# A rewritten attention order, keys ahead of weights, and no repeated scores, in an attention and two-layer-expert kernel

## The chip, the cores and the metric

One core of one Trainium2 chip runs the kernel. The metric is the device time of one execution in microseconds (us); the median of 3 runs of the kernel before is 613.02 us (612.81 to 613.07). TensorE is PE in the profile, its weight loads PEld, VectorE DVE, ScalarE ACT, GpSimd POOL, and SyncE, which issues most transfers, SP.

## The reference

```
scores = (q @ k.T) / sqrt(64)             # 2 batches, 8 heads, 576 positions, 64 per head
keep a score where 0 <= row - column < 64
attn = exp(scores - max) / (sum + 1e-9)
x    = attn @ v                           # as 1152 rows of 512
out1 = sum over 4 experts of p[:, e] * (relu(x @ w1[e]) @ w2[e])      # 512 -> 1024 -> 512
out  = g(out1 @ w_in) @ w_out             # 512 -> 2048 -> 512, g(h) = max(h, 0) + alpha * min(h, 0)
```

## The kernel before, in words

Queries are handled in 18 blocks of 64 positions, all 8 heads at a time. Block j passes through steps, each named by a letter and the block in one long string, `TABLE` (L767): **S** multiplies queries by the keys of this block and the one ahead of it (`att_S`, L322, 16 PE instructions); **M** adds the mask and takes the row's maximum on DVE (`att_M`, L337); **E** is the exponential on ACT, four instructions that also leave the row sums (`att_E`, L344); **N** adds the sums, takes the reciprocal and scales (`att_N`, L349 to L353), the scaling on DVE for the blocks in `SCALE_V` and on POOL for the rest; **PT** transposes on PE and copies out of PSUM (`att_PT`, L360, the copy by DVE for the blocks in `COPY_V`, by ACT for the rest); **PV** multiplies by the values (`att_PV`, L377) and writes the result as a high and a low part, for the blocks in `DIRECT` by ACT and DVE, for the rest by a DVE copy and two POOL operations (L390, L391).

Every large product is made of three products of such high and low parts. **W_f** splits column block f of the first weights, the high part on ACT (L231), the low one on POOL (L232); **V_f** does so for the second weights on ACT and DVE (L222, L215). **L_c_f** is one piece of the first layer of expert 0 on row chunk c (`l1_chunk`, L521, 12 matmuls), **B_c_t** one piece of its second layer (`l2_chunk`, L554, 12 matmuls). The string sets the order on every engine: each engine gets its share of the steps in the order of the words, and executes them in that order. After the string come chunk 3 and all other expert halves; there PE's first product is `product` (L451).

Two things in it are there beside the reference's work. `repeat` (L300) issues scores that are overwritten afterwards, as `REPEAT = {("S", 1): 2, ("PT", 0): 6}` says: 8 matmuls ahead of S_1 and 12 ahead of PT_0 (L307). And the transfers at the start stand in one list (L696 to L716): SP issues queries, four value blocks, the first weights as one transfer of 1 MB (`load_w`, L147), then the other keys; ACT's queue issues the keys of blocks 0 to 3. A transfer on SP waits for the one eight before it to land.

Of the kernel before, what the change touches and what calls it, by code (L numbers as in the profile page):

```python
# [8 lines left out]
F32 = mybir.dt.float32  # L9
# [17 lines left out]
def tile_kernel(ctx, tc, q, k, v, probs, w1, w2, w_in, w_out, alpha, out):  # L27
    nc = tc.nc


    B, S, H, D = v.shape
    NP = H // 2
    NT, DM = out.shape
    E, _, F = w1.shape
    F2 = w_in.shape[1]
    BLK = 64
    GRP = 192
    GB = GRP // BLK
# [60 lines left out]
    for c in range(1, NCH):  # L99
        n = CHUNK[c + 1] - CHUNK[c]  # L100
# [3 lines left out]
    denom = [ab.tile([P, NP, 2], F32, name=f"su{i}") for i in range(4)]  # L104
# [11 lines left out]
    def keys(j):  # L116

        return BLK if j % NB == 0 else P

    def load_q(g, a=0, z=GB):  # L120
        b, i = divmod(g, S // GRP)
        nc.sync.dma_start(out=qs[g % 3][:, a:z], in_=q[b, i, :, a:z])

    def load_k(b, a, z, queue=nc.sync):
        queue.dma_start(out=kts[b][:, a:z], in_=k[b, :, a:z])

    def load_v(j):

        b, i = divmod(j, NB)
        t = ab.tile([P, H, D], F32, tag="v", bufs=6, name=f"v{j}")  # L130
        if i == 0:
            nc.sync.dma_start(out=t[0:BLK], in_=v[b, 0:BLK])
        else:
            nc.sync.dma_start(out=t, in_=v[b, BLK * (i - 1):BLK * (i + 1)])
        v_t[j] = t

    def load_w(tid):
        which, s = tid
        if which == 0:
            late["raw0"] = sb.tile([P, KD, LEN[0]], F32, tag="ws", bufs=2, name="xs0")  # L140
            return
        convert(NF * (2 * (s - S1) + which))
        t = sb.tile([P, 4, FS], F32, tag="ws", bufs=2, name=f"ws{which}_{s}")
        if s < S1:
            e, o = divmod(s, SPE)
            src = w1[e][:, o * FS:(o + 1) * FS] if which == 1 else w2[e][o * FS:(o + 1) * FS, :]
            nc.sync.dma_start(out=t, in_=src.rearrange("(k p) f -> p k f", p=P))  # L147
        else:
            nc.sync.dma_start(out=t, in_=conv[tid])
        ws_t[tid] = t  # L150
# [17 lines left out]
    A11, A12, A22, SA1, SA2, SA3, SA4 = range(7)  # L168

    def w_block(s, u, i, j):  # L170
        t = ws_t[1, s]
        if s >= S1:
            return t[:, 2 * u + i, 2 * j * P:2 * (j + 1) * P].rearrange("p (k m) -> p k m", k=2)
        c = (2 * u + i) * P
        return t[:, 2 * j:2 * j + 2, c:c + P]
# [16 lines left out]
    def w_split(s, u, part):  # L192
        if (s, u) not in wf_t:
            wf_t[s, u] = [late["wfp"].tile([P, 7, 2, P], F32R, tag=f"wf{w}", bufs=2, name=f"wf{w}_{s}_{u}") for w in "hl"]
        hi, lo = wf_t[s, u]
        if part == A11:
            n, t = 2, ws_t[1, s]
            src = (t[:, 2 * u, :].rearrange("p (k m) -> p k m", k=KD) if s >= S1 else t[:, :, 2 * u * P:(2 * u + 1) * P])
        elif part == A22:
            n, src = 1, w_block(s, u, 1, 1)  # L200
        else:
            n, src = 4, sr_t.pop((s, u)).rearrange("p o k m -> p (o k) m")
        split(*[x[:, part:part + n].rearrange("p o k m -> p (o k) m") for x in (hi, lo)], src)
# [137 lines left out]
    def att_E(j):  # L341
        (pt, st, sm), w = p_t[j], keys(j)
        for hp in range(NP):
            nc.scalar.activation(out=pt[:, hp, 0:w], in_=sm[:, hp, 0:w], func=AF.Exp, scale=-1.0,  # L344
                                 bias=st[:, 0, hp:hp + 1], accum_out=denom[j % 4][:, hp, 0:1])

    def att_N(j):
        (pt, st), w = p_t[j][0:2], keys(j)
        nc.vector.tensor_reduce(out=st[:, 1, :], in_=denom[j % 4], op=ALU.add, axis=AX.X)  # L349
        nc.vector.reciprocal(out=st[:, 2, :], in_=st[:, 1, :])  # L350
        x, y = pt[:, :, 0:w], st[:, 2, :].unsqueeze(2).to_broadcast([P, NP, w])
        e = nc.vector if j in SCALE_V else nc.gpsimd
        e.tensor_tensor(out=x, in0=x, in1=y, op=ALU.mult)  # L353
# [339 lines left out]
        nc.scalar.activation(out=raw2(p)[:, :, t * P:(t + 1) * P], in_=ps.rearrange("p (k t) -> p k t", k=KD), func=AF.Copy)  # L693

    with tc.manual_schedule():
        for g, x, y in ((0, 0, 1), (0, 1, GB), (1, 0, 1)):  # L696
            load_q(g, x, y)
            load_k(0, g * GB + x, g * GB + y, nc.scalar)
        for su in denom:
            nc.vector.memset(su[:, :, 1:2], 1e-9)  # L700
        make_mask()
        load_v(0)
        load_v(1)
        make_identity(nc, ident)
        load_v(2)
        load_v(3)
        load_w((1, 0))
        load_q(1, 1, GB)
        load_k(0, GB + 1, 2 * GB)
        load_k(0, 2 * GB, NB)  # L710
        load_q(2)
        load_w((2, 0))
        load_v(4)
        load_v(5)
        nc.sync.dma_start(out=praw, in_=probs)
        nc.sync.dma_start(out=alph, in_=alpha)  # L716
# [275 lines left out]
```

## Time and profile before

| | |
|---|---|
| median of 3 runs | 613.02 us (612.81 to 613.07) |
| span of the profiled execution, first to last instruction | 610.7 us |
| the median less that span, time around it | 2.3 us |
| PE busy in it | 603.0 us (99%) |
| DVE, ACT, POOL busy | 483.2, 322.8, 277.7 us |
| first matmul starts | 3.57 us |
| first `l1_chunk` matmul (L_0_0) starts | 18.17 us |
| first `product` starts, by the chain | 87.86 us |

Times within the execution count from the span's start. In a timeline or chain row the first number is the start, the second the duration, "xN" the number of merged instructions; a bracket tells how long the engine was idle before it and who ended that. [...]

### The profile page before, as it was taken

The page shows a single profiled execution, that of the slowest core. Times are in us where ns is not written, and L with a number is a line of the kernel's source. Part 1 is how long each engine was busy: PE and PEld are TensorE (multiplying, and loading weights), DVE is VectorE, ACT ScalarE, POOL GpSimd, SP SyncE. Part 2 cuts the span into 40 slices and gives each one's busy share as a digit, 9 for nine tenths or more (in the row PEclk, how much of TensorE's full clock was granted, in tenths as well). Part 3 has the DMA queues.
Part 4 walks back from the last instruction along what each step waited for, and adds up shares of the span by engine and source line. Part 5 has one row for each costly group of instructions (what it writes and reads, how often), then busy time and mean ns, then how long its engine had stood idle before and what let it go on. Part 6 is the DMA issues. An engine that isn't in the chain of part 4 may idle for free.

```text
span 610.7 us, 11051 instructions
## 1 busy us (share of the span) xinstructions
PE 603.0 (99%) x4096; PEld 548.4 (90%) x4096; DVE 483.2 (79%) x969; ACT 322.8 (53%) x805; POOL 277.7 (45%) x282
## 2 busy tenths in 40 slices
PE   7999999999999999999999999999999999999997
PEld 6998999889889889989989989989898988988987
DVE  5987497799798798798698698657968989766785
ACT  6975456436427426426515625536777653653750
POOL 4756411074253254265152452522755586664450
PEclk9999999999999999999999999999999999999999
DMA  8951005234234325324324323012302412310012
GB/s 321 329 201 36 1 1 170 72 105 164 97 103 156 94 96 172 106 71 171 104 95 150 120 87 104 17 70 80 128 1 78 152 48 80 119 45 1 2 52 105
DMA packets 31798, 62.61 MB, mean 103 GB/s; under 512 B 2432, under 2 KB 11904, under 8 KB 30720
## 3 DMA queue, kind: packets, MB, share of 16 engines
q1 hardware_dynamic: 31024, 61.25, 29.5%
q8 instruction: 32, 0.52, 0.4%
q10 hardware_dynamic: 720, 0.66, 0.3%
q14 instruction: 22, 0.18, 0.1%
HBM read 51.14 MB, written 10.75 MB: 101 GB/s over the span
## 4 chain that ended last, share of the span: by engine, by line
PE 98%; DMA 1%; DVE 1%; ACT 0%; POOL 0%; issue 0%; ACTq 0%; POOLq 0%
PE o L566 42%; PE X L451 23%; PE Z L451 12%; PE W L451 6%; PE h L521 4%; PE oc L554 4%; PE s L322 1%; PE pt L360 1%; PE pv L377 1%; PE mX L653 1%; PE x L692 1%; DMA kt<-in_k_dram 1%; PE mZ L653 0%; PE pt L307 0%; ACT p L344 0%; PE mW L653 0%
## 5 line engine op out<-in xcount | busy, mean ns | idle before, releaser
L566 PE MATMUL o<-w2h,hl 128*128 128x512 f32 x380 | 148.2, 390 | 0.0
L566 PE MATMUL o<-w2l,hh 128*128 128x512 f32 x380 | 148.2, 390 | 0.0
L566 PE MATMUL o<-w2h,hh 128*128 128x512 f32 x380 | 147.9, 389 | 0.0
L294 POOL TENSOR_TENSOR ct<-ct 128x512 f32<-128x512 f32 x32 | 44.3, 1383 | 117.9 <-DVE ct L293 53.6
L566 PEld LDWEIGHTS o<-w2h,hl 128*128 128x128 f32 x380 | 71.3, 188 | 15.8 <-POOL hl L547 0.7
L566 PEld LDWEIGHTS o<-w2l,hh 128*128 128x128 f32 x380 | 71.3, 188 | 14.2
L566 PEld LDWEIGHTS o<-w2h,hh 128*128 128x128 f32 x380 | 71.3, 188 | 14.2
L678 DVE SCALAR_TENSOR_TENSOR acc<-o,pn,acc 128x512 f32<-128x512 f32 x63 | 47.1, 747 | 38.9 <-PE o L566 38.7
L190 POOL TENSOR_TENSOR sr<-ws 128x256 f32<-128x256 f32 x44 | 41.0, 932 | 72.6 <-DVE wfl L215 61.5
L215 DVE SCALAR_TENSOR_TENSOR w2l<-ws,w2h 128x512 fp32r<-128x512 f32 x48 | 44.4, 935 | 17.9 <-ACT w2h L222 17.8
L451 PE MATMUL X<-xth,wfl 128*128 128x256 f32 (+1 forms) x264 | 56.8, 296 | 0.0
L451 PE MATMUL X<-xth,wfh 128*128 128x256 f32 (+1 forms) x264 | 56.6, 295 | 0.0
L451 PE MATMUL X<-xtl,wfh 128*128 128x256 f32 (+1 forms) x264 | 56.6, 295 | 0.0
L222 ACT ACTIVATE wfh<-sr 128x1024 fp32r<-128x1024 f32 x22 | 23.2, 1059 | 53.5 <-POOL sr L190 53.5
L295 POOL TENSOR_TENSOR ct<-ct 128x512 f32<-128x512 f32 x32 | 47.3, 1478 | 2.5
L282 ACT ACTIVATE ct<-wd 128x512 f32<-128x512 f32 x32 | 21.3, 667 | 47.7 <-DVE ct L288 47.7
L451 PEld LDWEIGHTS X<-xth,wfl 128*128 128x128 f32 x264 | 42.6, 190 | 0.0
L451 PEld LDWEIGHTS X<-xth,wfh 128*128 128x128 f32 x264 | 42.6, 190 | 0.0
L451 PEld LDWEIGHTS X<-xtl,wfh 128*128 128x128 f32 x264 | 42.6, 190 | 0.0
L451 PE MATMUL Z<-xth,wfl 128*128 128x320 f32 (+1 forms) x176 | 37.8, 296 | 0.0
L451 PE MATMUL Z<-xth,wfh 128*128 128x320 f32 (+1 forms) x176 | 37.7, 296 | 0.0
L451 PE MATMUL Z<-xtl,wfh 128*128 128x320 f32 (+1 forms) x176 | 37.7, 296 | 0.0
(209 smaller groups left out, 1426.1 us busy)
## 6 DMA issues: line engine op xcount, KB each, us to landing
ws<-in_moe_w_dram SPq DMA_DIRECT2D x16, 1024.0 KB, 5.9
wd<-in_moe_w_in_dram SPq DMA_DIRECT2D x16, 512.0 KB, 4.0
cv<-ct SPq DMA_DIRECT2D x32, 256.0 KB, 2.4
wd<-in_moe_w_out_dram SPq DMA_DIRECT2D x16, 512.0 KB, 3.6
ws<-cv SPq DMA_DIRECT2D x8, 1024.0 KB, 5.1
v<-in_v_dram SPq DMA_DIRECT2D x16, 256.0 KB, 5.7
out_dram<-acc SPq DMA_DIRECT2D x7, 256.0 KB, 2.0
q<-in_q_dram SPq DMA_DIRECT2D x4, 384.0 KB, 6.6
```

The lines of the kernel that those rows point to most:

```text
L190: e.tensor_tensor(out=t4[:, o], in0=x, in1=y, op=op)
L215: nc.vector.scalar_tensor_tensor(out=lv, in0=src, scalar=1.0, in1=hv.bitcast(F32), op0=ALU.mult, op1=ALU.subtract)
L222: nc.scalar.activation(out=hv, in_=src, func=AF.Copy)
L282: nc.scalar.activation(out=a, in_=top.bitcast(F32), func=AF.Abs, scale=LIFT)
L294: nc.gpsimd.tensor_tensor(out=y, in0=y, in1=e, op=ALU.mult)
L295: nc.gpsimd.tensor_tensor(out=y, in0=r, in1=y, op=ALU.add)
L322: nc.tensor.matmul(sv[hp][c, 0:w].rearrange("p (n t) -> p n t", t=BLK), lhsT=qs[g % 3][r, jb, hp, :], rhs=kts[b][r, lo:i + 1, hp, :], star ...
L451: nc.tensor.matmul(ps, lhsT=w[:, d, :], rhs=x[:, d, :], start=(first and m == 0), stop=(m == 5), skip_group_check=True)
L521: nc.tensor.matmul(ps, lhsT=w[:, d * P:(d + 1) * P], rhs=x[:, d, :], start=(m == 0), stop=(m == 3 * KD - 1))
L554: nc.tensor.matmul(ps, lhsT=h_c[c, f][a][:, t * P:(t + 1) * P], rhs=w_t[2, 0, f][b], start=(n == 0), stop=(n == 3 * NF - 1))
L566: nc.tensor.matmul(ps, lhsT=h_t[s, p, f][a][:, t * P:(t + 1) * P], rhs=w_t[2, s, f][b][:, cols], start=(n == 0), stop=(n == 3 * NF - 1))
L678: nc.vector.scalar_tensor_tensor(out=at, in0=ps, scalar=sc, in1=at, op0=ALU.mult, op1=ALU.add)
```

## The change

The order of the steps is a new string. No matmul is repeated. The sets are new: the scaling in N is on DVE for 11 blocks where it was for 4, the copy after PT on DVE for 5 where it was 6, `DIRECT` has 7 blocks where it had 9. For blocks 4, 13, 14 and 16 (`REDUCED`) ACT's exponentials leave no sums, and DVE adds 128x512 numbers in one instruction. The low part of W_3 is made by DVE. The transfers at the start follow a list of words: keys of blocks 4 and 5 come ahead of the weights, and the first weights in three pieces of 1, 1 and 2 column blocks. For that `w1` is laid out anew ahead of the launch, so that each column block of 128 stands in one run in each partition, as the weights of the last four stages already do.

```diff
-    COPY_V = (0, 1, 2, 4, 10, 12)
-    DIRECT = (0, 2, 3, 7, 11, 14, 15, 16, 17)
-    REPEAT = {("S", 1): 2, ("PT", 0): 6}
-    SCALE_V = (13, 14, 15, 17)
+    COPY_V = (0, 6, 13, 14, 15)
+    DIRECT = (2, 3, 5, 10, 11, 13, 16)
+    REPEAT = {}
+    SCALE_V = (0, 2, 3, 5, 9, 10, 12, 13, 15, 16, 17)
+    REDUCED = (4, 13, 14, 16)
+    LOW_V = (3,)
...
+    PIECES = ((0, 1), (1, 2), (2, 4))
+    def load_piece():
+        o, i = pieces.pop(0)
+        nc.sync.dma_start(out=o, in_=i)
...
+            if tid == (1, 0) and PIECES:
+                for f0, f1 in PIECES:
+                    pieces.append((t[:, f0:f1], src[:, f0:f1]))
...
-        src = ws_t[1, 0][:, :, f * P:(f + 1) * P]
+        src = ws_t[1, 0][:, f].rearrange("p (k m) -> p k m", k=KD)
         nc.scalar.activation(out=hv, in_=src, func=AF.Copy)
-        nc.gpsimd.tensor_tensor(out=lv, in0=src, in1=hv.bitcast(F32), op=ALU.subtract)
+        if f in LOW_V:
+            low(lv, src, hv)
+        else:
+            nc.gpsimd.tensor_tensor(out=lv, in0=src, in1=hv.bitcast(F32), op=ALU.subtract)
...
-                                 bias=st[:, 0, hp:hp + 1], accum_out=denom[j % 4][:, hp, 0:1])
+                                 accum_out=None if j in REDUCED else denom[j % 4][:, hp, 0:1])
...
+        if j in REDUCED:
+            nc.vector.tensor_reduce(out=denom[j % 4][:, :, 0:1], in_=pt[:, :, 0:w], op=ALU.add, axis=AX.X)
...
+        HEAD = "p_0_0_1 p_0_1_3 q_1_1_3 v_0 k_4_6 p_1_0_1 v_1 v_2 w q_2 w v_3 k_6_9 w v_4 u v_5 r"
...
-            "S_0 S_1 M_0 S_2 S_3 E_0 M_1 E_1 N_0 M_2 N_1 M_3 E_2 N_2 E_3 PT_0 PT_1 N_3 PV_0 W_0 PV_1 W_1 "
+            "S_0 S_1 M_0 E_0 S_2 M_1 N_0 E_1 M_2 E_2 N_1 PT_0 S_3 S_4 M_3 E_3 N_2 S_5 N_3 PT_1 PV_0 W_0 M_4 PT_2 "
```

On PE, between S_2 and the first value product. Before (the first two rows are the end of S_3, then the 12 repeated scores into PT_0's bank):

```order
L322 MATMUL s_0_208<-kt_103,q_110 64x128 x2
L322 MATMUL s_1_209<-kt_103,q_110 64x128 x2
L307 MATMUL pt_264<-kt_103,q_109 64x128 x12
L360 MATMUL pt_264<-ident,p_193 64x128 x4
L360 MATMUL pt_283<-ident,p_224 128x128 x4
L377 MATMUL pv_293<-ptr_281,v_137 64x64 x8
```

With the change (the first two rows are the end of S_2; of S_3, S_4 and S_5 one row of four each stands here):

```order
L333 MATMUL s_0_196<-kt_103,q_109 64x128 x2
L333 MATMUL s_1_197<-kt_103,q_109 64x128 x2
L373 MATMUL pt_234<-ident,p_187 64x128 x4
L333 MATMUL s_0_241<-kt_103,q_110 64x128 x2
L333 MATMUL s_0_251<-kt_103,q_110 64x128 x2
L333 MATMUL s_0_275<-kt_103,q_110 64x128 x2
L373 MATMUL pt_288<-ident,p_208 128x128 x4
L390 MATMUL pv_295<-ptr_239,v_141 64x64 x8
```

PT_0 now follows S_2 directly, and S_3, S_4 and S_5 stand behind it; S_0 to S_8, PT_0 to PT_3 and PV_0 to PV_3 are done ahead of the first L piece in both.

On POOL, its work up to the low part of W_2. Before:

```order
L353 TENSOR_TENSOR p_193<-p_193,st_192 128x4x64
L353 TENSOR_TENSOR p_224<-p_224,st_223 128x512
L353 TENSOR_TENSOR p_238<-p_238,st_237 128x512
L353 TENSOR_TENSOR p_248<-p_248,st_247 128x512
L232 TENSOR_TENSOR w1l_0_308<-ws_0_149,w1h_0_307 128x512
L390 CAST xah_80<-xr_84 128x4x64
L391 TENSOR_TENSOR xal_81<-xr_84,xah_80 128x4x64
L232 TENSOR_TENSOR w1l_1_326<-ws_0_149,w1h_1_325 128x512
L353 TENSOR_TENSOR p_367<-p_367,st_366 128x512
L232 TENSOR_TENSOR w1l_2_415<-ws_0_149,w1h_2_414 128x512
```

With the change:

```order
L366 TENSOR_TENSOR p_208<-p_208,st_207 128x512
L403 CAST xah_80<-xr_84 128x4x64
L404 TENSOR_TENSOR xal_81<-xr_84,xah_80 128x4x64
L243 TENSOR_TENSOR w1l_0_310<-ws_0_114,w1h_0_309 128x512
L403 CAST xah_80<-xr_84 128x4x64
L404 TENSOR_TENSOR xal_81<-xr_84,xah_80 128x4x64
L243 TENSOR_TENSOR w1l_1_388<-ws_0_114,w1h_1_387 128x512
L243 TENSOR_TENSOR w1l_2_406<-ws_0_114,w1h_2_405 128x512
```

Three of the four first scalings left POOL; two blocks' split into a high and a low part came to it, and the low parts of W_1 and W_2 stand behind each other.

On SP, the transfers of the start with the change (ws is the first weights, kt the keys):

```order
L124 DMA q_109<-in_q_dram 128x512
L124 DMA q_110<-in_q_dram 128x512
L134 DMA v_141<-in_v_dram 64x512
L127 DMA kt_103<-in_k_dram 128x512
L124 DMA q_110<-in_q_dram 128x256
L136 DMA v_146<-in_v_dram 128x512
L136 DMA v_148<-in_v_dram 128x512
L144 DMA ws_0_114<-in_moe_w_dram 128x512
L124 DMA q_111<-in_q_dram 128x768
L144 DMA ws_0_114<-in_moe_w_dram 128x512
L136 DMA v_153<-in_v_dram 128x512
L127 DMA kt_103<-in_k_dram 128x768
```

Before, the queries of block 3 (128x256) were the third transfer, and the keys of blocks 4 and 5 came behind the whole of ws.

## Rows read from the trace of the kernel before

**Rows 1.** The page: busy time of each engine, PE in 40 slices.
```profile
PE 603.0 (99%) x4096; PEld 548.4 (90%) x4096; DVE 483.2 (79%) x969; ACT 322.8 (53%) x805; POOL 277.7 (45%) x282
...
PE   7999999999999999999999999999999999999997
...
PEclk9999999999999999999999999999999999999999
```
**Rows 2.** Busy time by stretch (us of each engine, then granted clock).
```profile
0.00:88.00 88.00, 83.38 (x991) 74.71 (x992) 63.23 (x274) 59.18 (x211) 44.48 (x61) 1.00 0.44 154
```
**Rows 3.** The chain that ended last, 0 to 20 us (start, us, what).
```profile
1.18 3.67 DMA kt<-in_k_dram
...
4.89 3.10 PE s L322 x48
7.99 2.20 PE pt L307 x24
10.19 0.57 PE pt L360 x4
...
10.79 1.28 DVE ptr L364 x2
...
12.49 1.05 POOL p L353
...
13.59 0.66 PE pt L360 x4
...
15.32 1.66 ACT p L344 x8
...
18.17 1.66 PE h L521 x12
```
**Rows 4.** The same chain, 20 to 48 us: pieces of PE back to back.
```profile
20.27 2.88 PE h L521 x24
23.15 0.44 PE pt L360 x4
23.58 1.43 PE h L521 x12
25.02 1.08 PE pv L377 x32
...
27.95 1.11 PE s L322 x32
```
**Rows 5.** The same chain, 80 to 100 us.
```profile
87.86 1.43 PE X L451 x12
```
**Rows 6.** PE's groups by shape, 0 to 9.7 us (busy us, mean ns; idle before).
```profile
L322 PE MATMUL s<-kt,q 64*64 64x128 f32 x48 | 3.1, 425 | 0.2 <-DMA kt<-in_k_dram 0.2
```
**Rows 7.** PE's groups by shape, 9.7 to 88 us.
```profile
L322 PE MATMUL s<-kt,q 64*64 64x128 f32 x208 | 7.1, 274 | 0.0
```
**Rows 8.** DVE's timeline at N_0, 6.0 to 7.6 us.
```profile
6.91 0.16 DVE L349 TENSOR_REDUCE st<-su 128x4 f32<-128x8 f32 x1
7.10 0.18 DVE L350 RECIPROCAL st<-st 128x4 f32<-128x4 f32 x1
```
**Rows 9.** POOL's timeline, 7 to 22 us.
```profile
7.43 0.61 POOL L353 TENSOR_TENSOR p<-p,st 128x256 f32<-128x256 f32 x1 [4.44 <-DVE st L350]
8.60 1.04 POOL L353 TENSOR_TENSOR p<-p,st 128x512 f32<-128x512 f32 x1 [0.55 <-DVE st L350]
...
13.49 1.28 POOL L232 TENSOR_TENSOR w1l<-ws,w1h 128x512 fp32r<-128x512 f32 x1
14.71 0.40 POOL L390 CAST xah<-xr 128x256 fp32r<-128x256 f32 x1
15.19 0.73 POOL L391 TENSOR_TENSOR xal<-xr,xah 128x256 fp32r<-128x256 f32 x1
```
**Rows 10.** DVE's, then ACT's groups by shape, 0 to 70 us.
```profile
L353 DVE TENSOR_TENSOR p<-p,st 128x512 f32<-128x512 f32 x4 | 2.9, 712 | 0.1
...
L387 DVE COPY xr<-pv 128x256 f32<-128x256 f32 x9 | 3.7, 415 | 0.0
...
L344 ACT ACTIVATE p<-sm,st 128x128 f32<-128x128 f32 x64 | 24.8, 389 | 0.9 <-DVE st L337 0.9
...
L222 ACT ACTIVATE w2h<-ws 128x512 fp32r<-128x512 f32 x4 | 2.4, 620 | 0.0
L231 ACT ACTIVATE w1h<-ws 128x512 fp32r<-128x512 f32 x4 | 2.4, 620 | 0.0
```
**Rows 11.** PE's waits, 0 to 88 us (total us, times, longest).
```profile
PE s L322 <- DMA kt<-in_k_dram: 3.8, 2, 3.6
```
**Rows 12.** DMA issue rows: values issued at 3.9 us, weights at 4.9 us.
```profile
v<-in_v_dram SPq DMA_DIRECT2D x1, 256.0 KB, 4.7
ws<-in_moe_w_dram SPq DMA_DIRECT2D x1, 1024.0 KB, 7.3
```

More of the change, by code (lines that the diff above doesn't have):

```diff
@@ L33, in tile_kernel @@
     NT, DM = out.shape
-    E, _, F = w1.shape
+    E, F = w1.shape[:2]
     F2 = w_in.shape[1]
@@ L135, in load_v @@
         v_t[j] = t
+    pieces = []
+    PIECES = ((0, 1), (1, 2), (2, 4))
+    def load_piece():
+        o, i = pieces.pop(0)
+        nc.sync.dma_start(out=o, in_=i)
     def load_w(tid):
@@ L145, in load_w @@
             e, o = divmod(s, SPE)
-            src = w1[e][:, o * FS:(o + 1) * FS] if which == 1 else w2[e][o * FS:(o + 1) * FS, :]
-            nc.sync.dma_start(out=t, in_=src.rearrange("(k p) f -> p k f", p=P))
+            src = (w1[e][o * FS:(o + 1) * FS] if which == 1 else w2[e][o * FS:(o + 1) * FS, :]).rearrange("(k p) f -> p k f", p=P)
+            if tid == (1, 0) and PIECES:
+                for f0, f1 in PIECES:
+                    pieces.append((t[:, f0:f1], src[:, f0:f1]))
+            else:
+                nc.sync.dma_start(out=t, in_=src)
         else:
@@ L170, in w_block @@
     def w_block(s, u, i, j):
[L171 to L175, printed above, removed]
+        return ws_t[1, s][:, 2 * u + i, 2 * j * P:2 * (j + 1) * P].rearrange("p (k m) -> p k m", k=2)
     def w_sums(s, u, e):
@@ L196, in w_split @@
         if part == A11:
-            n, t = 2, ws_t[1, s]
-            src = (t[:, 2 * u, :].rearrange("p (k m) -> p k m", k=KD) if s >= S1 else t[:, :, 2 * u * P:(2 * u + 1) * P])
+            n, src = 2, ws_t[1, s][:, 2 * u, :].rearrange("p (k m) -> p k m", k=KD)
         elif part == A22:
@@ L229, in split_w1 @@
         hv, lv = [x.rearrange("p (k m) -> p k m", k=KD) for x in w_tiles(1, 0, f)]
-        src = ws_t[1, 0][:, :, f * P:(f + 1) * P]
+        src = ws_t[1, 0][:, f].rearrange("p (k m) -> p k m", k=KD)
         nc.scalar.activation(out=hv, in_=src, func=AF.Copy)
-        nc.gpsimd.tensor_tensor(out=lv, in0=src, in1=hv.bitcast(F32), op=ALU.subtract)
+        if f in LOW_V:
+            low(lv, src, hv)
+        else:
+            nc.gpsimd.tensor_tensor(out=lv, in0=src, in1=hv.bitcast(F32), op=ALU.subtract)
     def split_w2(s, f):
@@ L343, in att_E @@
         for hp in range(NP):
-            nc.scalar.activation(out=pt[:, hp, 0:w], in_=sm[:, hp, 0:w], func=AF.Exp, scale=-1.0,
-                                 bias=st[:, 0, hp:hp + 1], accum_out=denom[j % 4][:, hp, 0:1])
+            nc.scalar.activation(out=pt[:, hp, 0:w], in_=sm[:, hp, 0:w], func=AF.Exp, scale=-1.0, bias=st[:, 0, hp:hp + 1],
+                                 accum_out=None if j in REDUCED else denom[j % 4][:, hp, 0:1])
     def att_N(j):
         (pt, st), w = p_t[j][0:2], keys(j)
+        if j in REDUCED:
+            nc.vector.tensor_reduce(out=denom[j % 4][:, :, 0:1], in_=pt[:, :, 0:w], op=ALU.add, axis=AX.X)
         nc.vector.tensor_reduce(out=st[:, 1, :], in_=denom[j % 4], op=ALU.add, axis=AX.X)
@@ L695, in tile_kernel, with head @@
     with tc.manual_schedule():
-        for g, x, y in ((0, 0, 1), (0, 1, GB), (1, 0, 1)):
-            load_q(g, x, y)
-            load_k(0, g * GB + x, g * GB + y, nc.scalar)
+        def head(item):
+            kind, *a = item.split("_")
+            a = [int(x) for x in a]
+            if kind == "p":
+                load_q(*a)
+                load_k(0, a[0] * GB + a[1], a[0] * GB + a[2], nc.scalar)
+            elif kind == "q":
+                load_q(*a)
+            elif kind == "k":
+                load_k(0, *a)
+            elif kind == "v":
+                load_v(*a)
+            elif kind == "w":
+                load_piece()
+            elif kind == "u":
+                load_w((2, 0))
+            elif kind == "r":
+                nc.sync.dma_start(out=praw, in_=probs)
+                nc.sync.dma_start(out=alph, in_=alpha)
+        HEAD = "p_0_0_1 p_0_1_3 q_1_1_3 v_0 k_4_6 p_1_0_1 v_1 v_2 w q_2 w v_3 k_6_9 w v_4 u v_5 r"
+        load_w((1, 0))
+        HEAD = HEAD.split()
+        for item in HEAD[0:3]:
+            head(item)
         for su in denom:
@@ L701, in tile_kernel @@
         make_mask()
-        load_v(0)
-        load_v(1)
         make_identity(nc, ident)
[L705 to L716, printed above, removed]
+        for item in HEAD[3:]:
+            head(item)
         def att_step(op, j):
@@ L978 @@
             a = _np.ascontiguousarray(a.reshape(-1, 128, a.shape[1]).transpose(1, 0, 2))
+        elif name == "moe_w1":
+            e, d, f = a.shape
+            a = _np.ascontiguousarray(a.reshape(e, d // 128, 128, f // 128, 128).transpose(0, 3, 2, 1, 4).reshape(e, f, d))
         elif name == "moe2_alpha":
```

14 rows, old and new, of the table TABLE are left out of this document.

## The prediction

> **What bounds the kernel now.** I read the page first: PE is busy 603.0 of 610.7 us, and the only slices under 9 tenths are the first and the last [rows 1]. So time can be won where PE works without need or waits, and that is at the start. The stretch from 0 to 88 us says how much room the others have: DVE 63.2, ACT 59.2, POOL 44.5 busy of 88 [rows 2]. Then the chain of waits from 0 to 20 us [rows 3]. The reader is to see three things in it. PE starts when the keys land (at 3.57 us, as the table of the profile says; S_1's keys at 1.18 + 3.67 = 4.85). From 7.99 it runs 2.20 us of repeated scores. And from 10.8 to 18.17 the chain leaves PE again and again (a copy on DVE, a scaling on POOL 1.05, exponentials on ACT 1.66): up to the first L piece the small engines set the pace. After that, chain and PE are the same thing, piece behind piece [rows 4], until the first product at 87.86 [rows 5], and PE has no other wait of size [rows 11]: of the 3.8 us of its largest, 3.6 are the start. The order of PE behind 87.86 is not touched, so what the change wins or loses by then it keeps to the end.
>
> One more reading: in the first 9.7 us a score matmul took 425 ns, later 274 [rows 6, 7]. [...]
>
> **The change part by part.** I walk the new PE order up to the second L piece, since S_0 to S_8, PT_0 to PT_3 and PV_0 to PV_3 stand ahead of the first L piece in both orders. [...]
>
> *Repeats away.* The 8 ahead of S_1 ran in the wait for its keys: nothing. The 12 ahead of PT_0 stood in the chain: 2.2 us of PE work less [rows 3].
>
> *What is late next: PT_0's own scaling.* N_0's reciprocal ended at 7.10 + 0.18 = 7.28 behind M_1 on DVE [rows 8], and its scaling took POOL 0.61 from 7.43 [rows 9]. It moves to DVE: half of 712 ns [rows 10] gives 0.36, so PT_0 can start at 7.65. S_1 and S_2, cold, end at 4.89 + 2.0 = 6.9. **A gap of about 0.8 us** opens on PE that the repeats used to fill.
>
> *PE from there.* PT_0 (0.8 at the lower level) to 8.45, S_3 to 9.45, then at the higher level from 9.7: S_4 and S_5 to 10.8, three more PT and four PV (1.3 + 2.2) to 14.3, S_6 to S_8 (1.65) to 15.9. Two short waits on scalings and copies add 0.4: 16.3, where the trace has 18.17. S_3 to S_5 need keys 4 and 5 and the queries of block 3 early. Values of 256 KB each, issued at 3.9, landed 4.7 us later, the 1 MB of weights issued at 4.9 landed 7.3 later [rows 12]: 1.05 MB in 12.2 - 8.6 = 3.6 us, 0.29 MB a us at the least. About 1.6 MB go out with and ahead of the last of the three, of which 0.77 MB (first keys and queries of blocks 0 to 2) have landed by 4.85; the rest takes 2.9 us at that rate and lands at 7.75. S_3 starts at 8.45: hidden, with 0.7 us left.
>
> *Then POOL holds the second piece.* PV_0's copy leaves DVE at about 13.0, behind N_3. POOL then does 0.40 + 0.73, the low part of W_0 1.28, again 0.40 + 0.73, the low part of W_1 1.28 [rows 9], with gaps of some 0.1: 17.9 to 18.0. So the first piece may start at 16.3 but L_0_1 not before 17.95, against 20.27 in the trace [rows 4]; PT_4 (0.44), done by then before, is still to come. **Gain so far 20.27 - 17.95 - 0.44 = 1.9 us.**
>
> *Layout and pieces.* ACT's split of the first weights, read in four runs of 128, took 620 ns, that of the second, read in one, 620 too [rows 10]: the layout changes nothing on ACT, nor is POOL near the bound after 88 us. Two more transfers on SP cost issue time that lies beside others.
>
> *DVE instead of POOL and ACT.* Seven more scalings on DVE at 0.71, one low part and four reductions of 512 numbers (no such row; between the 0.16 of a small one [rows 8] and 0.71 for 512 numbers in and out [rows 10], I take 0.6, nearest in size), less one copy and two DIRECT blocks' second pass (0.415): some 6.5 us more, on 63.2 of 88 [rows 2]. Covered on the average. An exponential without a sum must take no more than 389 ns [rows 10]; as a gain I count at most half, 4 x 4 x 0.19 = 3 us of ACT, off the path except for E_4. Behind L_0_1 I find one scaling left on POOL that PE waits for (N_6, its sums late on ACT), and two very short ones: 0.45 us lost, bounded by nothing and by two scalings on POOL, 2 x 1.05.
>
> *Bias of the walk.* The same walk through the old order comes out 0.3 us ahead of the trace at 20 us, since it leaves out small waits. I take it off. That leaves 1.9 - 0.45 - 0.3 = 1.15 us.
>
> *The clock.* The old PE came to the higher level while it ran without a gap since 4.89. The new one has the gap of 0.8 before PT_0. If the level rises at 9.7 all the same, nothing is lost; each microsecond that it comes later does half a microsecond of work less, and short waits take up a little: 0.45 us per us. I take the gap's 0.8 to 0.9 as the delay: 0.4 us. The trace cannot show the delay itself; its bounds are none and the whole stretch up to the L pieces (16.5 us: 6.8 x 0.45 = 3.1 us).
> [...]
>
> *Sum.* 1.15 - 0.4 = 0.75 us: **613.02 - 0.75 = 612.3 us**. The profiled span would go from 610.7 to about 609.95, with 2.3 around it as in the median.
>
> **The rivals.** What a measurement of this kernel can tell from no change is 0.2%, 1.2 us: below 611.8 is faster, above 614.2 slower.
> 1. *Faster: the new order leaves no wait.* Rise at 9.7 or before, POOL's chain and N_6 covered: 0.4 + 0.45 + 0.3 come back and half of L_0_1's wait more, 611.0. For it: DVE and ACT have 25 us each free up to 88 us [rows 2]. Against it: four steps of POOL in a row stand before L_0_1 whatever DVE does.
> 2. *Slower: the clock stays low through the first blocks.* Place: PE from 9.7 to the first L piece at 16 to 17 us. Price: 6.8 us at half rate, 3.1 us, on the 1.15 won: 613.0 - 1.15 + 3.1 = 615.0. It turns slower once the rise comes after some 15 us. For it: the work that held PE busy before the rise was largely the repeats (2.2 of 4.8 us [rows 3]). Against it: from 7.65 on, PE at the lower level would have no gap of its own for 8 us.
> 3. *The rise comes some 3 us late*, between forecast and rival 2: 3.4 x 0.45 = 1.5, so 613.4, no change. It differs from the forecast in size only.
> 4. *Keys or queries come later than S_3.* If the short list of transfers shares its rate with those behind it, S_3 waits up to 1 us: 613.3. Or the string moves no bound at all: 613.0.
>
> **How the numbers follow.** Forecast 0.35, rival 1 0.27, rival 2 0.2, rival 3 0.12, rival 4 0.06. The forecast's own range is 611.5 to 613.1, and a sixth of it lies below 611.8; so faster 0.27 + 0.06 = 0.33, slower 0.2 and a little of rival 3: 0.22, the same 0.45. The range takes in rival 1 and most of rival 2, up to where the rise comes at the first L piece: 610.9 to 614.9.
>
> **What the changed profile would show.** No 12 matmuls before PT_0 and a PE gap of about 0.8 ending near 7.65; score matmuls of 425 ns give way to 274 at a time to be read; the first L matmul near 16.5, the second piece ended by POOL's low part near 18; the first product near 87.1. DVE busy by some 6 us more up to 88. The prediction is wrong in its mechanism if PE waits on DVE in several places after 20 us, or if the stretch behind the first product changes.

## The result, and the profile after

The changed kernel took **616.43 us** (median of 4 runs, 615.74 to 616.68); the kernel before, on the same chip, 612.95 (four runs, 612.81 to 613.07). The ratio is 1.0054, 95% interval 1.0042 to 1.0066: slower by 3.5 us. The prediction said 612.3, between 610.9 and 614.9: wrong by more than its range, and on the other side.

The two profiled executions differ by 4.2 us (spans 614.9 and 610.7). The page of the changed kernel, busy time, PE in 40 slices and granted clock, to be read against [rows 1]:

```profile
PE 605.7 (99%) x4056; PEld 547.4 (89%) x4056; DVE 488.2 (79%) x978; ACT 321.5 (52%) x788; POOL 272.5 (44%) x278
...
PE   6999999999999999999999999999999999999997
...
PEclk9999999999999999999999999999999999999999
```

PE is busy 2.7 us *longer* with 40 matmul records less (20 matmuls of the code; a score matmul is two records, as the x24 for the 12 ahead of PT_0 in [rows 3] shows). The loss is not idle time. The chain that ended last, 0 to 17 us (start, us, what), which answers to [rows 3]:

```profile
1.18 3.94 DMA kt<-in_k_dram
...
5.16 1.14 PE s L333 x16
...
7.58 0.43 DVE p L366
...
8.15 1.03 PE pt L373 x4
9.18 2.77 PE s L333 x48
11.95 1.04 PE pt L373 x4
13.00 0.95 PE pv L390 x16
13.95 0.59 PE pt L373 x4
```

The repeats are gone and PT_0 starts at 8.15 (forecast 7.65) behind its own scaling. PE's pace is to be read from the pieces, since the clock line shows 9 throughout: a PT takes 1.03 at 8.15, 1.04 at 11.95, and 0.59 from 13.95 on. PE works at the slow pace (a score matmul of 423 ns) up to some 13.7 us and at the fast one (278 ns) from there; before, the slow pace (425 ns) had ended at 9.7 and the fast one (274) begun [rows 6, 7]. The prediction and the expectations call these the lower and the higher level of the clock, and the change from one to the other the rise. That is a reading of mine; no trace shows the clock change there: the granted clock is 1.00 on both sides of it in both traces (0 to 16 us before, 3.5 to 18.8 with the change).

PE's timeline where the first L pieces stand (start, us; in brackets idle time and what ended it); PE's list of waits from 17 to 92 us has these two and no other:

```profile
18.80 0.71 PE L534 MATMUL h<-xah,w1l 128*128 128x256 f32 x4 [0.16 <-DVE xr L400]
...
22.13 0.39 PE L534 MATMUL h<-xah,w1l 128*128 128x256 f32 x1 [0.22 <-POOL w1l L243]
```

The first L piece starts at 18.80, before at 18.17 [rows 3]: the whole new start costs only 0.63. The wait of 0.16 stands ahead of it; from there to the first product PE waits 0.22 us in all. And yet the chain reaches the first product late (before 87.86 [rows 5]):

```profile
34.64 0.60 PE s L333 x16
35.24 0.62 PE pv L390 x16
35.85 0.60 PE s L333 x16
36.45 0.59 PE pt L373 x4
...
92.08 1.43 PE X L464 x12
```

From the first L piece to the first product: 92.08 - 18.80 = 73.28 us; before, 87.86 - 18.17 = 69.69. That is **3.59 of the 4.2 us, in a stretch with the same pieces and next to no waits**. The rows show where: a lone S takes 0.60, a lone PT 0.59, a lone PV 0.62. Before, two S took 1.11, two PV 1.08 [rows 4]. The new string lets scores, transposes and products with the values alternate; the old one puts them in pairs. Behind the first product the offset stays at 4.2 to the end.

A busy time that grows while the mean of one matmul stays is the sign of this. The same 52 transposes from 17 to 92 us, before and with the change (busy us, mean ns):

```profile
L360 PE MATMUL pt<-ident,p 128*128 128x128 f32 x52 | 7.3, 278 | 0.0
...
L373 PE MATMUL pt<-ident,p 128*128 128x128 f32 x52 | 8.2, 280 | 0.0
```

**Theory (switch theory):** each change of kind between neighbours on PE costs 0.1 to 0.2 us. **Rival A:** the loss is the start's, a late rise and missing repeats. **Rival B:** waits on DVE, ACT or POOL at the heads of the pieces. From the first L piece to the end of the string before (B_2_1), the old string changes kind 28 times, the new one 47 times. The profile also gives the tile of the array that a matmul takes: 128*128 for PT, L and B, 128*64 for PV, 64*64 for S. Changes of that shape are 18 and 35. (Block 9, narrower than the rest, has a PT of 128*64 and a PV of 64*64; it is counted with the others here.)

In what follows, "start" is the start of the first L piece and "string" the time from it to the first product, each from a kernel's own trace (18.17 and 69.69 before).

### The profile page after: what moved, and what is told of

It reads as the page before. It is cut to its first block, busy times and chain, and to the rows that moved or that the text cites. A ratio compares the mean times of both kernels' runs of the same rounds, so it can differ in the third digit from the quotient of the medians.

```text
span 614.9 us, 10938 instructions
## 1 busy us (share of the span) xinstructions
PE 605.7 (99%) x4056; PEld 547.4 (89%) x4056; DVE 488.2 (79%) x978; ACT 321.5 (52%) x788; POOL 272.5 (44%) x278
## 4 chain that ended last, share of the span: by engine, by line
PE 97%; DVE 1%; DMA 1%; ACT 0%; POOL 0%; issue 0%; ACTq 0%; POOLq 0%
PE o L579 42%; PE X L464 23%; PE Z L464 11%; PE W L464 6%; PE oc L567 4%; PE h L534 4%; PE pt L373 2%; PE pv L390 2%; PE s L333 1%; PE mX L666 1%; DMA kt<-in_k_dram 1%; PE x L705 1%; PE mZ L666 0%; PE mW L666 0%; POOL w1l L243 0%; DVE sm L348 0%
```

## Experiments: is it the string, and is it the alternation

**The old start with the new string.** Transfers, repeats and order of the kernel before up to L_0_0, the engines of the first blocks with them; the new string behind.

```diff
-    REPEAT = {}
+    REPEAT = {("S", 1): 2, ("PT", 0): 6}
...
-    PIECES = ((0, 1), (1, 2), (2, 4))
+    PIECES = ()
...
-            "S_0 S_1 M_0 E_0 S_2 M_1 N_0 E_1 M_2 E_2 N_1 PT_0 S_3 S_4 M_3 E_3 N_2 S_5 N_3 PT_1 PV_0 W_0 M_4 PT_2 "
+            "S_0 S_1 M_0 S_2 S_3 E_0 M_1 E_1 N_0 M_2 N_1 M_3 E_2 N_2 E_3 PT_0 PT_1 N_3 PV_0 W_0 PV_1 W_1 PT_2 "
```

> The transfers, the repeated scores and the order up to the first L piece of the kernel before, and from there the string of the changed kernel; the weights keep their new layout but come in one transfer. Switch theory: 615.5 to 616.5, with the clock's rise near 9.7 as in the kernel before. Rival A (start and clock): 612.8 to 613.5. Rival B (waits on DVE, ACT or POOL that the new string adds): as by the switch theory in time, but with more than 2 us of waits of PE between 20 and 88 us.

615.12 us (615.00 to 616.36), ratio 1.0043 (1.0030 to 1.0055), 0.4 under what was expected of the switch theory. Three rows of its chain:

```profile
18.98 4.55 PE h L534 x36
...
25.41 0.44 PE pt L373 x4
...
91.69 1.43 PE X L464 x12
```

String 72.71, 3.02 above the old one. PE's only wait from 17 us on, 0.3 on DVE, ends where the string starts. Rival A falls for the larger part, rival B for this string; 3.02 / 17 more changes of shape = 0.18 each.

The string of the changed kernel is 0.57 longer than this one, and that stands at its head: there PT_5 is reached 7.02 us behind the first L piece (18.80 to 25.82), here 6.43 us behind it (18.98 to 25.41). It is the stretch with the wait of 0.22 for POOL's low part.

```profile
25.82 0.44 PE pt L373 x4
```

**The kernel before, alternating.** Only neighbours in its string change places.

```diff
-  PV_4 PV_5 S_9 Q_5 M_9 S_10 ... PT_6 PT_7 S_11 ... S_12
+  PV_4 S_9 Q_5 M_9 PV_5 S_10 ... PT_6 S_11 PT_7 ... S_12
...
-  PV_8 PV_9 S_13 ... S_14 ... S_15 PT_10 PT_11
+  PV_8 S_13 ... PV_9 S_14 ... PT_10 S_15 PT_11
...
-  PV_10 PV_11 S_16 S_17 PT_12 PT_13
+  PV_10 S_16 PT_12 PV_11 S_17 PT_13
...
-  PV_12 PV_13 PT_14 PT_15 ... PV_14 PV_15 PT_16 PT_17
+  PV_12 PT_14 PV_13 PT_15 ... PV_14 PT_16 PV_15 PT_17
```

> The kernel before, its start untouched; in the string behind the first L piece only neighbours change places, so that scores, transposes and products with the values alternate: 43 changes of kind in place of 28, the same pieces, repeats, transfers and engines. Switch theory: 15 x 0.1 to 0.2, so 614.5 to 616.0, with no added waits of size. Rival A (start and clock alone): 613.0 within 0.4. Rival B (waits): time lost, but then as idle time of PE ahead of the moved pieces with DVE or ACT as what ended it.

615.13 us (614.26 to 615.42), ratio 1.0033 (1.0021 to 1.0046), with start, engines and transfers of the kernel before. Its chain:

```profile
17.81 1.66 PE h L521 x12
...
46.66 0.62 PE pv L377 x16
47.27 0.60 PE s L322 x16
47.87 0.59 PE pt L360 x4
...
50.26 5.47 PE oc L554 x24
...
89.55 1.43 PE X L451 x12
```

String 71.74: 2.05 us more for 15 changes of shape, **0.14 each**. PE waits nowhere in it. The six pieces from 46.66 to 50.26 take 3.60; in the kernel before the same six, in pairs, run from 45.99 to 49.13 in its chain, 3.14. Where the time sits, the groups of weight loads of this kernel show, 36 to 60 us (busy, mean ns | idle before), first the kernel before, then this one:

```profile
L360 PEld LDWEIGHTS pt<-ident,p 128*128 128x128 f32 x25 | 2.7, 141 | 0.4 <-issue 0.3
L377 PEld LDWEIGHTS pv<-ptr,v 128*64 128x64 f32 x80 | 2.6, 137 | 0.6 <-issue 0.4
L322 PEld LDWEIGHTS s<-kt,q 64*64 64x64 f32 x80 | 2.2, 133 | 0.1
```
```profile
L360 PEld LDWEIGHTS pt<-ident,p 128*128 128x128 f32 x26 | 2.7, 140 | 1.0 <-issue 0.7 <-POOL xch L390 0.2
L377 PEld LDWEIGHTS pv<-ptr,v 128*64 128x64 f32 x80 | 2.7, 137 | 1.0 <-issue 0.5 <-DVE st L350 0.2
L322 PEld LDWEIGHTS s<-kt,q 64*64 64x64 f32 x80 | 2.2, 132 | 0.4 <-DVE xr L389 0.2
```

A weight load takes as long as ever (140, 137, 132 ns; before 141, 137, 133). But the loads stand idle 2.4 us in all, for the most part with nothing that they wait for ("issue"); in the kernel before, in the same window, 0.4 + 0.6 + 0.1 = 1.1. Where the lists of loads show a pause among these pieces, it stands ahead of the first load of one: 0.17 us ahead of a PV at 56.86 here; in the changed kernel 0.17 each ahead of S at 34.57, PV at 35.17, PT at 36.38 and PV at 36.97.

Some of that idle time is put down to other engines, so it could still be waits. The lengths say no: in the five traces with many lone pieces (the changed kernel with and without the repeats, this one, the one above and the next one) there are 47 lone PV of 128*64, and each takes 0.615 or 0.616 us from its start to that of the next piece, whatever stands beside it. Waits would scatter.

**The changed kernel with pairs.** Neighbours of one kind side by side again: 25 changes of shape in place of 35.

```diff
-  PT_4 L_0_3 ... PT_5 ... PV_4 S_9 PT_6 M_9 PV_5 N_8 B_0_1 E_9 PT_7
+  L_0_3 ... PT_4 PT_5 ... PV_4 PV_5 S_9 M_9 N_8 B_0_1 E_9 PT_6 PT_7
...
-  PV_6 M_10 S_11 E_10 PT_8 PV_7 M_11 S_12 N_10 PT_9
+  M_10 S_11 E_10 PV_6 PV_7 M_11 N_10 PT_8 PT_9 S_12
...
-  PT_10 M_14 S_15 PT_11 S_16 X_0 ... PV_10 N_14 PT_12 ... PV_11
+  M_14 PT_10 PT_11 S_15 S_16 X_0 ... PV_10 PV_11 N_14 PT_12 ...
```

> The changed kernel, its start untouched; in the string behind the first L piece neighbours of one kind are put side by side again: 36 changes of kind in place of 47, nothing else. Switch theory: 11 x 0.1 to 0.2 us less than the changed kernel, so 614.2 to 615.3. Rival A: 616.4 within 0.4. Rival B: no change, or slower where pieces are pulled ahead of the work they wait for.

615.80 us (615.63 to 616.32), ratio 1.0049 (1.0036 to 1.0061): next to nothing won, and above the 614.2 to 615.3 expected. The PT, PV and S pieces of its string are 1.16 us shorter together than in the changed kernel, for 10 changes fewer. But L pieces got 0.93 longer, and the list of PE's waits says why: L pieces wait 0.4 us for DVE's low part of a weight block and 0.2 each for two of POOL's.

The pairs were pulled ahead of the work that feeds them. A miss as an experiment, since two things changed; it shows the trade that a string makes.

**The same extra matmuls, in two places.** 24 repeated score matmuls more in the kernel before: between the two PT of six pairs, or ahead of six S pieces.

```diff
-    REPEAT = {("S", 1): 2, ("PT", 0): 6}
+    REPEAT = {("S", 1): 2, ("PT", 0): 6, ("PT", 7): 2, ("PT", 9): 2, ("PT", 11): 2, ("PT", 13): 2, ("PT", 15): 2, ("PT", 17): 2}
```
```diff
-    REPEAT = {("S", 1): 2, ("PT", 0): 6}
+    REPEAT = {("S", 1): 2, ("PT", 0): 6, ("S", 9): 1, ("S", 10): 1, ("S", 11): 1, ("S", 13): 1, ("S", 14): 1, ("S", 16): 1}
```

> The kernel before with 24 repeated score matmuls more, four each between the two transpose pieces of a pair (16 and 17, 14 and 15, and so on down to 6 and 7). The matmuls alone, at the 69 ns that a score matmul costs in a block of 8 in 0.55 us, are 1.65 us. Switch theory: 12 changes of kind more at 0.15 us, 1.8 us on top: 616 to 616.6. Rival A (the clock alone): 614.5, as the next kernel. A third reading, that a piece costs more for being short and alone and not for the change of kind, gives the same here as the switch theory.

> The same 24 repeated score matmuls more, but each four of them ahead of a score piece, so that no change of kind is added. All theories: 1.65 us more than the kernel before, 614.3 to 614.7. The switch theory needs this kernel to be 1.2 to 2.4 us below the one with the same matmuls between transposes; rival A needs the two equal.

617.74 us between transposes (617.55 to 618.89, ratio 1.0084, 1.0069 to 1.0098), above its 616 to 616.6; 615.38 beside scores (615.00 to 617.37, 1.0044, 1.0029 to 1.0058). The medians are 2.4 us apart, which looks like 0.20 for each of 12 changes. But three things are mixed in that. The start of the second was late (19.72 against 18.01, its keys landed later), so by the strings, 74.72 and 71.34, the two are 3.38 apart. In both, PE pauses once within the PV pair ahead of the first B piece, with no releaser in the trace, and this costs 0.37 more in the first (PV pairs of 1.83 and 1.46 us, in the kernel before 1.08). And the work is not the same: `repeat` gets one PSUM tile from `att_PT` and two from `att_S`, so that by the code the same number of matmuls takes two places of the array or four. The traces show them starting by twos and by fours, a step of 0.11 us apart. Instructions at work in each 0.11 us from the start of one such piece, between transposes, then beside scores (the number behind the x):

```profile
43.13:43.24 0.11, 0.11 (x2) 1.00 1.05 410
43.24:43.35 0.11, 0.11 (x4) 1.00 1.55 559
...
49.97:50.08 0.11, 0.11 (x4) 1.00 0.00 0
50.08:50.19 0.11, 0.11 (x8) 1.00 0.00 0
```

So 8 instructions (4 matmuls of the code) need four steps of 0.11 us between transposes and two beside scores, 0.22 us more in each of six pieces, 1.3 in all. That leaves 3.38 - 0.37 - 1.3 = 1.7 us: **0.14 for each of 12 changes**, an estimate that agrees with the alternating kernel. That the string beside scores is longer by just the 1.65 us that the matmuls were priced at is luck: six times 0.22 are 1.3, and the pause in the PV pair makes up the rest. Two rows from the chains, eight instructions alone between transposes and eight within a run of scores:

```profile
27.36 0.58 PE pt L307 x8
...
28.27 0.22 PE s L307 x8
```

**Changes of kind without a change of shape.** The second PT of three pairs goes behind the L or B piece that follows: 34 changes of kind in place of 28, still 18 of shape.

```diff
-  PT_10 PT_11 M_15 E_14 N_13 N_14 L_1_1
+  PT_10 L_1_1 PT_11 M_15 E_14 N_13 N_14
...
-  PT_12 PT_13 X_1 ... B_1_0      PT_14 PT_15 N_17 X_3 L_2_0
+  PT_12 X_1 ... B_1_0 PT_13      PT_14 N_17 X_3 L_2_0 PT_15
```

> The kernel before, with the second transpose piece of three pairs moved behind the L or B piece that follows the pair (PT L PT L in place of PT PT L L): six changes of kind more, 34 in place of 28, all between pieces of 128*128 tiles. If every change of kind costs 0.15 us: 0.9 us more from the first L piece to the last L chunk, 53.9 in place of 53.0 us, and some 613.9. If only a change of the tile's shape costs: 52.7 to 53.1 us there and the time of the kernel before within 0.4 us.

613.03 us (11 runs, 612.24 to 614.27), ratio 1.0001 (0.9993 to 1.0010). In its trace one S piece ahead of the edit waited for keys, which makes its string 0.7 longer; so I count from PT_10, the first row here, to the first product:

```profile
41.06 0.59 PE pt L360 x4
41.64 1.42 PE h L521 x12
43.07 0.44 PE pt L360 x4
...
88.33 1.43 PE X L451 x12
```

47.27 us; in the kernel before, from PT_10 at 40.66 to 87.86, 47.20. Six changes inside 128*128 cost nothing: a PT behind an L piece takes 0.44, no more than the second of a pair. To stand alone does not cost by itself either. **What costs is the change of tile shape**, and the theory is narrowed to that.

Block 9 sharpens it, in traces that are already here. The first row is PT_8 and PT_9 of the kernel before, 128*128 and 128*64, between a B and an L piece; the others are from the changed kernel, PV_8 and PV_9 (128*64 and 64*64) and a pair of PV of 128*64, both behind an L piece:

```profile
35.81 0.87 PE pt L360 x8
...
41.46 1.23 PE pv L390 x32
...
63.85 1.08 PE pv L390 x32
```

PV_8 and PV_9 are of one kind and differ in shape, and cost 0.15 more. PV_9 and S_13, of two kinds but both 64*64, cost nothing side by side: in the kernel before PV_8, PV_9 and three S take 2.54 us (38.12 to 40.66), less than 1.23 and the 1.47 of three S in a row. But the change from 128*128 to the 128*64 of PT_9 and back is free: 0.87 is twice the 0.44 of a PT among L pieces. So the shape that the profile prints is not the whole condition. By the code PV and S put successive matmuls on different parts of the array and PT_9 does not; whether that is the difference was not tried. Counted by what costs, the new string has 18 changes more than the old one and the alternating one 13: 0.17 and 0.16 us each.

## Experiments: what the start is worth

**Only the repeats taken away, and only the repeats put back.** The kernel before with `REPEAT = {}`; the changed kernel with the old line.

```diff
-    REPEAT = {("S", 1): 2, ("PT", 0): 6}
+    REPEAT = {}
```
```diff
-    REPEAT = {}
+    REPEAT = {("S", 1): 2, ("PT", 0): 6}
```

> The kernel before with its 20 repeated score matmuls taken out and nothing else. Theory of two parts: PE idles ahead of PT_0, the rise of the clock comes at 12 to 17 us, and the kernel takes 613.5 to 615. If the repeats are mere work in the chain (the prediction's first term): 610.8 to 611.8.

> The changed kernel with one thing put back: the 20 repeated score matmuls ahead of S_1 and PT_0. Theory of two parts (changes of kind in the string, and a clock that rises 2 to 7 us later without the repeats): the rise is back at 9.5 to 10 us, the first L piece starts near 17.5 instead of 18.8, the string behind it takes what it does in the changed kernel (56.6 us to the first piece of the last L chunk): 614.6 to 615.8, that is 0.8 to 1.8 us less than the changed kernel. If switches are all of it: 616.4 or slower, since the repeats are 2.2 us of PE work.

Without repeats the kernel before took 613.44 us (11 runs, 612.41 to 614.44), ratio 1.0000 (0.9991 to 1.0009). Its profiled execution starts 0.97 later (19.14; S_1's scores, which wait for keys, start 0.63 later), the string is the same (69.63). So the 20 matmuls are worth half a microsecond at most there: the prediction's "2.2 us less" is not won, but neither is 1 to 2 us lost, as I now expected.

The changed kernel with them took 615.78 (615.52 to 616.37), ratio 1.0038 (1.0025 to 1.0050): about 1.0 us better than the changed kernel by the two ratios, whose intervals just overlap, though PE has more to do. Its chain, 5 to 13 us:

```profile
4.95 1.98 PE s L333 x32
6.93 2.47 PE pt L318 x24
9.41 0.56 PE pt L373 x4
9.96 1.47 PE s L333 x48
11.43 0.59 PE pt L373 x4
```

PE is at the fast pace by 9.4 (PT_0 takes 0.56, in the changed kernel 1.03), with no gap ahead of PT_0; S_3 to S_5 take 1.47 where the changed kernel needs 2.77. Start 17.57, 1.23 earlier, of which S_1's keys, landed 0.21 earlier, are a part; the string runs to 90.86, 73.29 us, the changed kernel's 73.28. **The loss of the string does not hang on the start.**

**The new start ahead of the old string.** Seven splices, with the seam at the first L piece, behind PT_5, behind the first B piece, and at the first L piece with the scaling of block 4 on DVE; three of them also with the repeats. The first and the last seam:

```diff
-  ... S_7 S_8 N_4 M_6 N_5 L_0_0 L_0_1 W_3 Q_4 V_0 L_0_2 ...
+  ... S_7 S_8 N_4 M_6 N_5 L_0_0 W_3 Q_4 PT_4 E_6 M_7 L_0_1 M_8 N_6 V_0 ...
...
+    SCALE_V = (0, 2, 3, 4, 5, 13, 14, 15, 17)
```

> The transfers, the layout, the absence of repeats and the order up to the first L piece of the changed kernel, and from there the string of the kernel before (28 changes of kind between the pieces of PE from the first L piece to the last B piece of the string, where the changed kernel has 47). Switch theory (each change of kind between pieces costs PE 0.1 to 0.2 us, and the start costs about 0.6): 613.0 to 613.9, first product near 88.5. Rival A (what the changed kernel lost came from its start: the late clock, the missing repeats): 616 to 616.5, as the changed kernel.

> The changed kernel (its transfers, no repeats) up to PT_5, so that each engine keeps the new order there, and from B_0_0 the string of the kernel before, with 27 changes of kind in place of 47. Switch theory: the start and the L pieces cost what they do in the changed kernel (PE some 1.1 us later than before at the first B piece), the string behind them what it does before: 613.6 to 614.4. Rival A: 616 to 616.5. In the splice at the first L piece, the wait on POOL for the scaling of block 4 (3.1 us) hid this.

> The same, with the repeated scores of the kernel before put back ahead of S_1 and PT_0 (20 matmuls). If the late rise of the clock is what the repeats prevented, the rise is back at 9.5 to 10 us, the first L piece starts 1 to 2 us earlier and the kernel takes 612 to 613.2, as fast as the kernel before or faster; if the repeats only cost PE time, it is 0.5 to 1.5 us above the kernel without them, 614.2 to 615.8.

> The changed kernel up to its first B piece, where the products with the values of blocks 4 and 5 wait for nothing in its trace, and from there the string of the kernel before (28 changes of kind in place of 47); no repeats; the scaling of block 7 on DVE. Theory of two parts: start 0.6 to 2 us later than before (late rise), string as before: 613.6 to 615.0. If instead the waits behind the start come back (scalings of blocks 6 and 7 on POOL): idle PE of 1 us or more near 30 us, and the time says nothing on the string.

> The same with the 20 repeated matmuls put back, the version that the theory of two parts makes the best: rise at 9.5 to 10 us, first L piece near 17.5 (18.2 in the kernel before), 53 to 53.6 us from there to the first piece of the last L chunk: 612.0 to 613.2, as fast as the kernel before or half a microsecond faster, and 3 to 4 us faster than the changed kernel.

> The changed kernel (no repeats) up to its first L piece, then the string of the kernel before, as in the first splice, but with the scaling of block 4 on DVE. Theory of two parts: first L piece at 18 to 20 us as the clock rises, string 53.0 to 53.6 us: 612.8 to 614.8; the wait of 3.1 us on POOL is gone. If the new start costs the string more than that (DVE or POOL late on the splits of the first weights), 615 or more, with those waits in the trace.

> The same with the 20 repeated score matmuls: rise near 10 us, first L piece at 17.5 to 18.2, string 53.0 to 53.6 us: 612.2 to 613.2, and the best of the kernels here with the new start. If it beats the kernel before, then by 0.6 us at most.

| seam, repeats | us (median) | ratio, interval | start | PE's waits behind the seam |
|---|---|---|---|---|
| first L piece, none | 618.90 | 1.0094 (1.0076 to 1.0112) | 20.05 | POOL p 3.1 |
| behind PT_5, none | 617.73 | 1.0078 (1.0064 to 1.0091) | 20.18 | ACT ptr 2.0 |
| behind PT_5, with | 618.11 | 1.0092 (1.0067 to 1.0116) | 17.54 | ACT ptr 2.0, DVE st 1.3, POOL p 0.8 |
| first B piece, none | 615.48 | 1.0032 (1.0020 to 1.0043) | 18.53 | DVE acc 0.8, DVE ptr 0.7 |
| first B piece, with | 614.73 | 1.0021 (1.0012 to 1.0030) | 18.18 | DVE acc 0.8, DVE ptr 0.7 |
| first L, block 4 on DVE, none | 617.64 | 1.0070 (1.0057 to 1.0083) | 17.96 | DVE st 2.7, DVE p 0.7 |
| the same, with | 618.65 | 1.0091 (1.0076 to 1.0106) | 17.31 | DVE st 3.1, DVE p 0.7 |

All seven missed the time of their theory, each with waits of the kind named in its row (for two of them the expectation had named such waits as the other outcome): two tables that each feed PE in time do not do so when joined. In the five with a wait of 2 us or more the granted clock fell as well: in the clock line of each, one slice of 40 reads 7 or 8 in place of 9, in the other two none (last section). None beats the kernel before. What they do show is behind the seam. From PT_8 to the first product the old string takes 52.05 us, within 0.01, in all seven, and 52.05 in the kernel before. In these eight traces the price of that string is set by its order; nothing that happened earlier changed it.

## Why the prediction was wrong

- **The step that failed: the prices of a piece in the walk, S 0.55, PT 0.44 and PV 0.54.** These came from [rows 4], where pieces stand in pairs, and I used them for an order in which they stand alone; of the string behind L_0_1 I priced nothing but POOL's waits, as if its order were free. Measured: lone pieces of 0.60, 0.59 and 0.62, and 3.59 us more in the string. The old start with the new string puts 3.02 of that down to the order alone: 17 more changes of shape at 0.18; counted by what costs, 18 changes at the 0.16 of the alternating kernel are 2.8 to 2.9, and the rest of 0.1 to 0.2 I cannot divide further. The other 0.57 stands at the first L pieces, where PE waits 0.22 us for POOL.
- The same price fell on the start. "Three more PT and four PV (1.3 + 2.2)" are 3.5; at the fast pace, in the changed kernel with its repeats, PT_1 to PV_3 run from 11.36 to 15.88, 4.52. Of that, 0.4 is a wait of PEld for ACT's copy (PEld pv <- ACT ptr), for which the forecast had its 0.4 for short waits; 0.6 is the lone pieces. No run shows the 0.8 of PT_0 "at the lower level": it took 1.03, at 8.15.
- **The late rise ("The clock"): right in kind, too small.** Forecast 0.4 us for a delay of the rise by 0.8 to 0.9. The rise came at 13.7, four later, and put back with the repeats it is worth some 1.0, by the first L piece (1.23 less 0.21 for earlier keys, if those pass through in full) and by the two ratios. That is rival 3, "the rise comes some 3 us late", which I gave 0.12; rival 2's 3.1 us was not reached. The rate of the forecast, half a microsecond of work lost per microsecond, is near what the runs show: S_3 to S_5 take 2.77 at the slow pace and 1.47 at the fast one, so a slow microsecond does 0.47 less. That the delay is as long as the gap was an estimate of mine, and no run shows it: behind a gap of 1.0 us ahead of PT_0 the rise came at 13.7 here, 13.1 in the splice at the first B piece, and not before 17.1 in the one behind PT_5 (last section).
- *Repeats away, 2.2 us in the chain:* wrong as a gain. PE filled the time at the slow pace (without the repeats a matmul of a 128*128 PT takes 435 ns up to 13 us, against 279 from 0 to 88 us with them), and the kernel before without repeats is no faster.
- *Gap ahead of PT_0:* right, 1.0 us to 8.15 (0.8 to 7.65 forecast; S_1's keys landed 0.27 later and the scaling took 0.43, not 0.36).
- *Keys of blocks 4 and 5 hidden:* right. S_3 follows PT_0 at 9.18 without a wait.
- *L_0_1 at 17.95, held by POOL:* wrong in time, since PE itself came to L_0_0 only at 18.80. POOL's low part holds L_0_2 instead, by 0.22.
- *DVE covered:* right. Up to the first product DVE is busy 68.5 us of 92 (63.2 of 88 [rows 2]), 5.3 more where 6.5 were forecast, and PE waits for it 0.2 us behind 17 us. Layout and pieces: nothing in the trace speaks against zero; they were not tried alone.
- The signs I named for a wrong mechanism, waits on DVE after 20 us and a change behind the first product, both stayed away. The one that spoke was the date of the first product, 92.08 in place of 87.1: every sign I had chosen was a wait, and the loss is none.

Added up on the spans: forecast -0.75, measured +4.2, 4.95 apart. At the first L pieces the forecast was -1.2 (1.9 less bias and clock) and +0.63 came, 1.8 apart: some 0.6 for the rise (1.0 in place of 0.4), 0.3 for the keys of S_1, 0.7 for the pieces from PT_1 to the first L piece (6.2 us at the fast pace, from 11.36 to 17.57, in place of 5.5); 0.2 remain. In the string 0.45 was forecast and 3.59 came, 3.1 apart. That the total missed the range and not only the forecast is the string's doing; by the start alone the kernel would have taken some 613.6 (612.95 + 0.63, an estimate).

On weight loads: from 36 to 60 us of the kernel before those of the L pieces, of one shape from matmul to matmul, stand idle 0.0 us. In the same window those of the PV of 128*64 stand idle 0.6 and those of the PT of 128*128 0.4, while those of PT_9 (128*64), behind PT_8, stand idle 0.0. What it is in a change of shape that costs, no run here shows.

## What to carry to other kernels

When an order of small matmuls is rewritten, price a piece by what stands ahead of it: on PE, a run of one tile shape was cheap here (two PV 1.08, two lone ones 1.23) and each change of shape cost 0.14 to 0.18 us, so counting the changes of shape (18 against 35) would have forecast most of this result. When the same work is moved to another place as a test, look whether it still runs at the same pace there. Compare the time of the same pieces between two landmarks, not only the waits: a loss inside "busy" has no releaser, and shows as a busy sum that grows while the mean of one matmul stays. An interleaving that avoids waits must save more than its changes of shape cost, and pairs pulled ahead of their feed give the gain back.

## What was not expected of the hardware

- **A change of tile shape cost PE 0.14 to 0.18 us in these runs; a change of operand inside 128*128 cost nothing (47.27 us against 47.20, with six more), and neither did the 128*64 of PT_9 beside 128*128 (0.87 for the two PT).** Why the loads stand idle at a change that costs stays open: only the order was varied, not the shapes themselves.
- **The same start does not give the same rise.** Six kernels here run the changed kernel's start without repeats. Read from the length of the pieces in one execution of five of them, the rise lies between 11 and 12 us in two (the one with pairs, and the splice with block 4 on DVE, where PT_1 takes 0.59 at 11.86 and 11.91), between 13 and 14 in two (13.7 in the changed kernel, 13.1 in the splice at the first B piece), and not before 17.1 in the splice behind PT_5. There the pieces from PT_1 to PT_3 still take 1.04 to 1.06 each, two of them here:

```profile
11.88 1.05 PE pt L373 x4
...
15.02 1.05 PE pv L390 x16
```

  The sixth, the splice at the first L piece, starts its first L piece as late as this one (20.05 and 20.18). With the repeats S_3 to S_5 take 1.47, the fast pace, in the changed kernel (from 9.96) and in the splice at the first B piece (from 10.57). What the repeats brought in these two is a rise at the same place, more than a shorter time.
- **A wait in the middle cost more than itself.** In the splice with block 4 on DVE, PE waited 2.7 us up to 32.4. Busy time by stretch of 4 us (PE, PEld, DVE, ACT, POOL, then the granted clock):

```profile
30.00:34.00 4.00, 1.62 (x26) 1.32 (x28) 2.39 (x7) 3.69 (x18) 2.92 (x4) 0.77 0.25 83
34.00:38.00 4.00, 4.00 (x39) 3.46 (x36) 3.26 (x25) 1.92 (x9) 1.37 (x3) 0.81 1.00 381
38.00:42.00 4.00, 4.00 (x23) 3.40 (x23) 2.14 (x6) 0.29 (x1) 2.04 (x2) 1.00 0.59 225
```

  The granted clock is 0.77 and 0.81 in the two stretches from the wait on, with PE busy throughout the second, and full again after 38 us (1.00). The pieces right behind the wait are long: one S takes 1.13 and two PV 1.90, where a lone S took 0.60 and two PV 1.08.

```profile
32.38 1.13 PE s L333 x16
33.51 1.90 PE pv L390 x32
```

  In the splice behind PT_5, where PE had waited 2.0 us for ACT's copy, the clock line reads 8 in its third slice (30.9 to 46.3 us). A seam with 3.4 us of waits (2.7 and 0.7) cost 5.6 us of string (75.3 against 69.7).
